# An order model that waits for the eighth-preceding transfer, and keeps a lock for each of two engines (linear attention and MLP, one core)

## Chip, cores and metric

The kernel runs on one core of one Trainium2 chip. The metric is the device time of one execution in microseconds (us). Before the change the median of three runs was 403.05 us (402.95 to 403.12).

The engines are named as in the profile: PE is TensorE (PEld its weight loads), DVE is VectorE, ACT is ScalarE, POOL is GpSimd, SP is SyncE, which here issues nearly all transfers (DMA).

## What is computed

A block whose output is the input plus two branches of its normalised form: linear attention with 32 heads of 16, and an MLP with squared ReLU. The sequence is 2048 long, the width 512, the MLP's width 1376; all is f32.

```python
def _A_ref(x, wqkv, wo):                    # q, k, v: (heads, S, 16)
    ...
    phi = lambda t: jnp.where(t > 0, t + 1, jnp.exp(t)) + 1e-6
    pq, pk = phi(q), phi(k)
    kv = jnp.einsum("bhsd,bhse->bhde", pk, v)
    z = jnp.einsum("bhsd->bhd", pk)
    num = jnp.einsum("bhqd,bhde->bhqe", pq, kv)
    den = jnp.einsum("bhqd,bhd->bhq", pq, z)[..., None] + 1e-6
    ...
def _B_ref(x, w1, b1, w2, b2):
    h = jnp.einsum("bsd,df->bsf", x, w1) + b1
    ...
    h = r * r                                # r = max(h, 0)
    out = jnp.einsum("bsf,fd->bsd", h, w2) + b2
...
x = A_x
xn = _layernorm(x, axis=-1)
return x + _A_ref(xn, A_wqkv, A_wo) + _B_ref(xn, B_w1, B_b1, B_w2, B_b2)
```

## The kernel before

**Work.** Tokens go in 16 tiles of 128, four to a block of 512. Each f32 product is made of a high and a low part of either operand and three matmuls, high by high, low by high and high by low; names that end in h and l are such parts (xs0h, xs1l, wkh, wkl). Most of the MLP is multiplied in a form with seven products in place of eight, for which sums and differences of weights are made on chip, written to DRAM (wd1, wd2, wdz) and read back (ops). In the first 105 us the 16 token tiles pass one after the other: statistics (st, mv, y) and normalisation (xp) on DVE, a turn of the tile, the key projection into PSUM (ps), phi of it (k, then pk, whose high half is made on ACT and whose low half on DVE), and the product of pk with the tokens, split into halves as well (tok, ACT and POOL), summed in acc. A number behind the name is that of the tile: k9 belongs to tile 9.

The first eight tiles are turned by TensorE and stored for later use (xTd, from t). The others take another way: DVE writes the normalised tiles of four (xp8, xp12), SP sends them through 16 small transfers to xg (xg8, xg12: each line of the order is 32 partitions by 512 numbers), and DVE turns each with a STREAM_TRANSPOSE into xT, whose halves are xs0h/xs0l or xs1h/xs1l. wv is the value weight, a megabyte, loaded through SP too.

**Order.** Nothing is issued when the program text runs. Each call on an engine is caught by a `Recorder` and kept by `Program.add` as a task with an estimated duration. `Program.order` (line 183) then searches for an order: `play` (line 269) runs a list scheduler over a model of the engines, in which each engine takes the ready task with the earliest due date; `press` (line 254) moves due dates ahead for tasks before which TensorE stood idle in the model; 500 such rounds run from each of the seven seeds in `STARTS`, and then the due dates of stretches of the results are crossed. `emit` (line 340) issues the tasks of the best order; so one line, 343, stands for all instructions in the profile. TensorE's own order is that of the text and is not searched; the first tasks of all engines (`fixed`) are as written, too.

Two things in the model matter here. `t.lock` marks sums (tensor_tensor and scalar_tensor_tensor on DVE without a PSUM operand, tensor_tensor on POOL): one number, `locked`, lets none of them start before the end of the last one, on whichever engine. And a transfer (`t.size` above 0) takes its place behind the previous ones in one stream, `dma`, and its readers wait for its landing, `t.lag` later. How many transfers are under way is not limited in the model. In the program as built each SP or ACT transfer signals one of eight semaphores, in turn, and waits for the one before it on the same semaphore.

Of the kernel before, what the change touches and what calls it, by code (L numbers as in the profile page):

```python
# [79 lines left out]
class Program:  # L80
# [96 lines left out]

    ENGINES = ("tensor", "vector", "scalar", "gpsimd", "sync")
    DEEP, FAR = 4.0, 15.0
    STARTS = (0, 1, 3, 5, 6, 7, 8)  # L180
    ROUNDS = 500

    def order(self):
# [36 lines left out]
        plain, best, found = [t.due for t in ts], None, []  # L220
        for start in self.STARTS:
            chance, back = random.Random(start), (8, 16, 4)[start % 3]
# [46 lines left out]
    def play(self):  # L269
        ts, engines, inf = self.tasks, self.ENGINES, float("inf")  # L270
        free = dict.fromkeys(engines, 0.0)
        later = {e: [] for e in engines}
        now = {e: ([], []) for e in engines}
        lane, at, before = self.lanes, dict.fromkeys(engines, 0), dict.fromkeys(engines)
        when = dict.fromkeys(engines, inf)
        locked, dma, last = 0.0, 0.0, 0.0
        push, pop = heapq.heappush, heapq.heappop

        def look(e):
            row = lane[e]  # L280
            if at[e] < len(row):
                t = row[at[e]]
                when[e] = inf if t.left else max(free[e], t.ready)
            elif now[e][0] or now[e][1]:
                when[e] = free[e]
            else:
                when[e] = max(free[e], later[e][0][0]) if later[e] else inf

        for t in ts:
            t.left, t.ready, t.cause = len(t.preds), 0.0, None  # L290
            if not t.left and not t.placed:
                push(later[t.engine], (0.0, t.index, t))
        for e in engines:
            look(e)
        done = 0
        while done < len(ts):
            e = min(engines, key=when.get)
            begin = when[e]
            if at[e] < len(lane[e]):
                t = lane[e][at[e]]  # L300
                at[e] += 1
            else:
                wait, (easy, hard) = later[e], now[e]
                while wait and wait[0][0] <= begin + 0.1:
                    t = pop(wait)[2]
                    push(hard if t.lock else easy, (t.due, t.index, t))
                if hard and (not easy or hard[0] < easy[0] and locked <= begin + 0.1):
                    t = pop(hard)[2]
                else:
                    t = pop(easy)[2]  # L310
                    if t.size and dma > begin + self.DEEP and t.due > begin + self.FAR:
                        push(wait, (dma - self.DEEP / 2, t.index, t))
                        look(e)
                        continue
            done += 1
            t.start, t.behind = max(begin, t.ready), before[e]
            before[e] = t
            if t.lock:
                t.start = max(t.start, locked)
                locked = t.start + t.dur  # L320
            end = t.start + t.dur
            free[e] = end - t.skip
            last = max(last, end)
            if t.size:
                dma = end = max(dma, end) + t.size / 300e3
            for s, lag in t.follow:
                ready = end + lag
                if ready >= s.ready:
                    s.ready, s.cause = ready, t
                s.left -= 1  # L330
                if not s.left:
                    o = s.engine
                    if not s.placed:
                        push(later[o], (s.ready, s.index, s))
                    if o != e:
                        look(o)
            look(e)
        return last
# [1384 lines left out]
```

## Time and profile before

| | before |
|---|---|
| median of three runs | 403.05 us |
| the profiled execution | 403.15 us |
| its span, first to last instruction | 401.3 us |
| granted TensorE clock, mean | 1.000 |
| PE busy | 393.5 us, 1769 matmuls, 98% |
| DVE busy | 351.0 us, 565 instructions, 87% |
| ACT busy | 271.7 us, 475 instructions, 68% |
| POOL busy | 59.1 us, 73 instructions, 15% |

A row of the timeline is read so: start and duration in us, engine, line, operation, output and inputs by the program's names (tile numbers left out), their shape and how many instructions the row stands for; in brackets how long the engine stood idle before it and what ended the wait. SPq is SP's queue while it issues a transfer. A row of the chain of waits is start, duration and what the time was spent on. The span leaves out 1.85 us of the profiled execution.

### The profile page before, as it was taken

What the parts mean: (1) busy time and instruction counts of PE and PEld (TensorE: products, weight loads), DVE (VectorE), ACT (ScalarE), POOL (GpSimd) and SP (SyncE); (2) the same over time, 40 slices, a digit from 0 to 9 for tenths busy, and PEclk for the clock granted to TensorE, in tenths of its full rate; (3) what the DMA queues carried; (4) which work ended last, traced back from release to release, by engine and by line L of the source; (5) the groups of instructions that cost most, each with busy time, mean ns of one, the idle gap of its engine ahead of it and who ended that gap; (6) DMA issues with size and microseconds to landing.
All of it is one profiled execution on the core that took longest, in us unless ns stands there. A gap on an engine that the chain in (4) does not pass through costs nothing.

```text
span 401.3 us, 5606 instructions
## 1 busy us (share of the span) xinstructions
PE 393.5 (98%) x1769; PEld 325.4 (81%) x1769; DVE 351.0 (87%) x565; ACT 271.7 (68%) x475; POOL 59.1 (15%) x73
## 2 busy tenths in 40 slices
PE   7999999999999999999999999999999999999994
PEld 6778887888888888888888888888888888888883
DVE  6899979899898999999889989988999989676884
ACT  5776776666769989999747552277958677455440
POOL 2232324540213424300000000030000000000000
PEclk9999999999999999999999999999999999999999
DMA  7872654876499898589446799989998599989434
GB/s 229 297 221 61 166 155 186 281 275 244 148 314 296 324 340 310 235 292 313 179 140 193 246 259 224 363 240 295 265 239 272 186 227 296 236 266 275 158 65 93
DMA packets 80177, 94.36 MB, mean 235 GB/s; under 512 B 39410, under 2 KB 50674, under 8 KB 79892
## 3 DMA queue, kind: packets, MB, share of 16 engines
q1 hardware_dynamic: 78964, 93.49, 76.0%
q10 hardware_dynamic: 1088, 0.26, 0.4%
q0 software_dynamic: 96, 0.26, 0.3%
q8 instruction: 14, 0.23, 0.2%
q14 instruction: 15, 0.12, 0.1%
HBM read 57.55 MB, written 34.34 MB: 229 GB/s over the span
## 4 chain that ended last, share of the span: by engine, by line
PE 86%; DVE 6%; DMA 3%; SPq 1%; issue 1%; ACT 1%; DVEq 0%; ACTq 0%
PE ps L343 50%; PE acc L343 36%; DMA wv<-in_A_wqkv_dram 2%; SPq L343 1%; DVE xp L343 1%; DVE st L343 1%; DVE y L343 1%; DMA x<-in_A_x_dram 1%; DVE xs0l L343 1%; DMA xg<-xp 0%; DVE pk L343 0%; DVE k L343 0%; DVE res L343 0%; DVE o L343 0%; DVE ops L343 0%
## 5 line engine op out<-in xcount | busy, mean ns | idle before, releaser
L343 PE MATMUL ps<-s,ops 128*128 128x512 f32 x429 | 101.0, 389 | 0.0
L343 PEld LDWEIGHTS ps<-s,ops 128*128 128x128 f32 x429 | 80.5, 188 | 16.7
L343 PE MATMUL acc<-s,ops 128*128 128x512 f32 (+1 forms) x222 | 51.0, 381 | 0.0
L343 ACT ACTIVATE s<-rr 128x512 fp32r<-128x512 f32 x56 | 34.9, 630 | 22.9 <-DVE s L343 10.9
L343 DVE TENSOR_TENSOR s<-rr,s 128x512 fp32r<-128x512 f32 x56 | 39.0, 706 | 10.5 <-ACT s L343 9.6
L343 PE MATMUL acc<-pk,tok 128*128 128x512 f32 x192 | 47.2, 394 | 0.2 <-ACT pk L343 0.2
L343 PEld LDWEIGHTS acc<-s,ops 128*128 128x128 f32 x222 | 40.5, 188 | 8.2 <-ACT s L343 0.3
L343 PEld LDWEIGHTS acc<-pk,tok 128*128 128x128 f32 x192 | 35.4, 188 | 8.5 <-POOL tok L343 0.6
L343 PE MATMUL acc<-T,ops 128*128 128x512 f32 x168 | 41.2, 389 | 0.0
L343 PE MATMUL ps<-T,ops 128*128 128x512 f32 x168 | 40.9, 390 | 0.0
L343 PEld LDWEIGHTS acc<-T,ops 128*128 128x128 f32 x168 | 31.5, 188 | 6.6
L343 PEld LDWEIGHTS ps<-T,ops 128*128 128x128 f32 x168 | 31.5, 188 | 6.5
L343 POOL TENSOR_TENSOR tok<-xp,tok 128x512 fp32r<-128x512 f32 x16 | 22.4, 1398 | 28.2 <-ACT tok L343 20.5
L343 PE MATMUL ps<-xs0h,ops 128*128 128x512 f32 x72 | 23.6, 389 | 0.0
L343 POOL TENSOR_TENSOR ops<-s,ops 128x512 fp32r<-128x512 f32 x12 | 16.7, 1395 | 36.6 <-ACT ops L343 36.2
L343 ACT ACTIVATE rr<-acc 128x512 f32<-128x512 f32 x23 | 13.5, 591 | 10.8 <-PE acc L343 10.8
L343 DVE STREAM_TRANSPOSE d<-d 128x1024 f32<-128x1024 f32 x16 | 19.8, 1236 | 0.2
L343 POOL DMA_DIRECT2D out_dram<-res x2 | 1.5, 729 | 122.5 <-DVE res L343 120.0
L343 PE MATMUL acc<-xs0h,ops 128*128 128x512 f32 x56 | 18.4, 389 | 0.0
L343 POOL TENSOR_TENSOR made<-t,made 128x512 fp32r<-128x512 f32 x2 | 3.1, 1559 | 98.5 <-issue 97.4
L343 ACT ACTIVATE rr<-rr,odds 128x512 f32<-128x512 f32 x15 | 10.8, 722 | 9.6 <-DVE rr L343 9.6
L343 DVE TENSOR_TENSOR rr<-acc,rr 128x512 f32<-128x512 f32 x21 | 14.3, 687 | 2.7 <-PE acc L343 1.3
(181 smaller groups left out, 811.7 us busy)
## 6 DMA issues: line engine op xcount, KB each, us to landing
ops<-wd SPq DMA_DIRECT2D x77, 256.0 KB, 4.6
wd<-ops SPq DMA_DIRECT2D x35, 512.0 KB, 3.7
ops<-wd SPq DMA_DIRECT2D x23, 512.0 KB, 5.9
wd<-ops SPq DMA_DIRECT2D x25, 256.0 KB, 4.0
res<-in_A_x_dram SPq DMA_DIRECT2D x32, 128.0 KB, 6.1
out_dram<-res SPq DMA_DIRECT2D x26, 128.0 KB, 3.5
ops<-wdz SPq DMA_DIRECT2D x6, 512.0 KB, 6.1
x<-in_A_x_dram SPq DMA_DIRECT2D x5, 512.0 KB, 6.2
```

The costliest lines, as they stand in the source:

```text
L343: getattr(getattr(self.nc, t.engine), t.name)(*map(real, t.args), **{k: real(a) for k, a in t.kw.items()})
```

## The change

The starts of the search go from seven seeds to one, another. The model's lock becomes one for each of the two engines, and a sum waits for the lock of the other engine alone, so that DVE's sums no longer wait in the model for each other. A transfer of SP or ACT does not start in the model before the eighth-preceding one has landed. The tasks, their number, their dependences and the order of TensorE are as before.

```diff
-    STARTS = (0, 1, 3, 5, 6, 7, 8)
+    STARTS = (2,)
...
-        locked, dma, last = 0.0, 0.0, 0.0
+        locked, dma, last = {"vector": 0.0, "gpsimd": 0.0}, 0.0, 0.0
+        other = {"vector": "gpsimd", "gpsimd": "vector"}
+        landed = [0.0] * 8
...
-                if hard and (not easy or hard[0] < easy[0] and locked <= begin + 0.1):
+                if hard and (not easy or hard[0] < easy[0] and locked[other[e]] <= begin + 0.1):
...
             if t.lock:
-                t.start = max(t.start, locked)
-                locked = t.start + t.dur
+                t.start = max(t.start, locked[other[e]])
+                locked[e] = t.start + t.dur
+            if t.size and e != "gpsimd":
+                t.start = max(t.start, landed[-8])
             end = t.start + t.dur
...
             if t.size:
                 dma = end = max(dma, end) + t.size / 300e3
+                if e != "gpsimd":
+                    landed.append(end + t.lag)
```

The diff tells nothing of the order that comes out. It differs on DVE, ACT, POOL and SP from about 24 us on, save the last dozen instructions of each. Three places follow; a number at a name's end counts tiles of the pool, and differs between the two programs without meaning.

DVE, around the keys of tile 9 (k9, pk9), beside the turning of tiles 12 and 13 (xT3 from xg12). Before:

```order
L343 STREAM_TRANSPOSE xT3_757<-xg12_624 128x4x4x32
L343 TENSOR_TENSOR ops_753<-t1_0_718,ops_753 128x2x256
L343 TENSOR_TENSOR xs1l_174<-xT2_636,xs1h_165 128x4x128
L343 TENSOR_TENSOR xs0l_404<-xT3_757,xs0h_393 128x4x128
L343 SCALAR_TENSOR_TENSOR k9_769<-ps3_70,k9_769 128x512
L343 STREAM_TRANSPOSE xT3_757<-xg12_624 128x4x4x32
L343 TENSOR_TENSOR t2_0_810<-raw_2_2_314 128x256
L343 SCALAR_TENSOR_TENSOR pk9_804<-k9_769,pk9_804 128x512
```

The same place now:

```order
L349 STREAM_TRANSPOSE xT3_760<-xg12_631 128x4x4x32
L349 TENSOR_TENSOR ops_427<-raw_2_1_306,ops_427 128x256
L349 TENSOR_TENSOR xs1l_174<-xT2_652,xs1h_165 128x4x128
L349 SCALAR_TENSOR_TENSOR k9_771<-ps3_70,k9_771 128x512
L349 TENSOR_TENSOR xs0l_402<-xT3_760,xs0h_392 128x4x128
L349 STREAM_TRANSPOSE xT3_760<-xg12_631 128x4x4x32
L349 SCALAR_TENSOR_TENSOR pk9_793<-k9_771,pk9_793 128x512
```

k9 moved ahead of the xs0l sum, and the sum behind the first transpose is another, of half the size. On ACT, pk9's high half now follows k9 at once; before, tok11 stood between them. On DVE near 24 us (not shown) one of two BN_AGGR that stood ahead of xp4's normalisation moved behind it, beside the other.

SP, from the stores of the turned tiles 4 to 7 (xTd1) to the first stores of made weights (wd2_1). Before:

```order
L343 DMA xTd1_78<-t4_400 512x1x128
L343 DMA xg8_474<-xp8_429 32x512 x16
L343 DMA xTd1_78<-t5_472 512x1x128
L343 DMA wv_604<-in_A_wqkv_dram 128x4x512
L343 DMA xg12_624<-xp12_575 32x512 x4
L343 DMA xTd1_78<-t6_549 512x1x128
L343 DMA xg12_624<-xp12_575 32x512 x12
L343 DMA xTd1_78<-t7_628 512x1x128
L343 DMA wd2_1_87<-ops_421 128x512 x2
```

Now:

```order
L349 DMA xTd1_78<-t4_399 512x1x128
L349 DMA xTd1_78<-t5_472 512x1x128
L349 DMA xg8_503<-xp8_430 32x512 x16
L349 DMA xTd1_78<-t6_544 512x1x128
L349 DMA xg12_631<-xp12_564 32x512 x16
L349 DMA xTd1_78<-t7_621 512x1x128
L349 DMA wd2_1_87<-ops_419 128x512 x2
L349 DMA wv_746<-in_A_wqkv_dram 128x4x512
```

wv moved from between xg8 and xg12 behind both, and the store of t5 ahead of xg8. On DVE the first xp8 normalisations, which xg8 reads, stand later: a statistics instruction (BN_STATS) for tile 7 and one for tile 12, xs0l and k4 are now ahead of the second of them.

ACT, in the MLP, around the relu and square of one tile (c21, then s0_2_1, its high half). Before:

```order
L343 ACTIVATE h0_1498<-h0_1498 128x512
L343 ACTIVATE ops_1554<-raw_1_4_1253 128x256
L343 ACTIVATE c21_2_1566<-ps0_67,odds_105 128x512
L343 ACTIVATE c21_2_1566<-c21_2_1566 128x512
L343 ACTIVATE rf2_1434<-ps1_68 128x512
L343 ACTIVATE s0_2_1_1581<-c21_2_1566 128x512
```

Now:

```order
L349 ACTIVATE h0_1498<-h0_1498 128x512
L349 ACTIVATE d1_1555<-rr0_1_1294,odds_105 128x512
L349 ACTIVATE c21_2_1562<-ps0_67,odds_105 128x512
L349 ACTIVATE ops_1566<-raw_1_4_1258 128x256
L349 ACTIVATE c21_2_1562<-c21_2_1562 128x512
L349 ACTIVATE rf2_1438<-ps1_68 128x512
L349 ACTIVATE s0_2_1_1581<-c21_2_1562 128x512
```

The 128x256 copy (ops from raw) moved from ahead of the relu to behind it, and d1, which came later, stands ahead of it.

## The prediction

> **What bounds the kernel now.** I read the page's busy times first, where TensorE is busy for 98% of the span, then busy time by stretch of the span.
>
> ```profile
> PE 393.5 (98%) x1769; PEld 325.4 (81%) x1769; DVE 351.0 (87%) x565; ACT 271.7 (68%) x475; POOL 59.1 (15%) x73
> ```
>
> ```profile
> 7.70:66.00 58.30, 58.13 (x266) 46.97 (x265) 52.71 (x113) 41.51 (x87) 19.77 (x30) 1.00 0.62 189
> 66.00:70.00 4.00, 3.78 (x17) 2.80 (x17) 3.90 (x9) 3.62 (x7) 0.36 (x1) 1.00 0.20 81
> 70.00:150.00 80.00, 80.00 (x370) 66.65 (x369) 72.72 (x109) 62.69 (x109) 24.07 (x20) 1.00 0.80 277
> ...
> 395.90:401.30 5.40, 0.02 (x1) 0.00 (x0) 0.95 (x3) 0.20 (x1) 0.00 (x0) 0.98 0.49 97
> ```
>
> The columns are the stretch, its length, then busy time and count for PE, weight loads, DVE, ACT and POOL, the granted clock, the DMA share and GB/s. From 7.70 to 395.90 TensorE has work without a visible hole but for 0.17 us before 66 and 0.22 us behind it; the stretches left out read like that of 70 to 150, full. The clock is 1.00 in all of them, so it leaves nothing to win. VectorE is 87% busy and never the bound in a whole stretch. TensorE's order is fixed, so the body can give back only the moments at which an operand came late. A shared row of matmuls hides small ones, because each matmul is drawn longer than its place in the pipeline. The chain of waits gives the step: a row of twelve in 2.72 us is 0.227 each. With it the PE timeline can be checked for lateness:
>
> ```profile
> 69.67 2.72 PE ps L343 x12
> ```
>
> ```profile
> 24.98 1.07 PE L343 MATMUL ps<-wkh,xs1l 128*128 128x512 f32 x4
> 26.22 0.66 PE L343 MATMUL ps<-ident,xp 128*128 128x128 f32 x4 [0.17 <-DVE xp L343]
> ...
> 65.38 1.07 PE L343 MATMUL ps<-wkh,xs1l 128*128 128x512 f32 x4
> 66.67 3.00 PE L343 MATMUL acc<-pk,tok 128*128 128x512 f32 x12 [0.22 <-ACT pk L343]
> 69.51 0.39 PE L343 MATMUL ps<-wkh,xs1h 128*128 128x512 f32 x1
> ...
> 149.07 0.39 PE L343 MATMUL ps<-xs1h,ops 128*128 128x512 f32 x1
> 149.30 3.01 PE L343 MATMUL acc<-s,ops 128*128 128x512 f32 x12
> 152.15 1.07 PE L343 MATMUL ps<-T,ops 128*128 128x512 f32 x4
> ```
>
> The four matmuls from 65.38 are over at 65.38 + 4 × 0.227 = 66.29; the next block starts at 66.67, **0.38 late**, and takes 69.51 − 66.67 = 2.84 instead of 2.72, another 0.12: **0.50 us** together, the largest stall of the body. At 26.22 it is 26.22 − 25.89 = 0.33. The block at 149.30 takes 2.85, 0.13 too long. What else I find by this step are four single delays of about 0.1 before 22 us, where the orders of both programs agree. All in all, 0.50 + 0.39 (26.22 and its short block) + 0.13 + 0.4, they come to some 1.4 us: the most that a new order can win in the body. It can lose without such a bound.
>
> **The change part by part.** No instruction is added or removed, and the order of the matmuls is the same; the eight semaphores on which transfers really wait are in both programs, so the eighth-preceding wait is new in the model alone and has no cost on the chip. [...] What changes are rows on DVE, ACT, POOL and SP. The first rows (to about 24 us) and the last dozen of every engine are word for word alike, so the 7.7 us at the start and the 5.4 us at the end stay.
>
> *The stall at 66.67.* What came late there:
>
> ```profile
> 45.60 7.48 DMA wv<-in_A_wqkv_dram
> ...
> 58.73 1.97 DMA xg<-xp
> ```
>
> ```profile
> 60.82 0.71 DVE L343 STREAM_TRANSPOSE xT<-xg 128x512 f32<-128x512 f32 x1 [1.78 <-DMA xg<-xp]
> ...
> 61.00 1.29 POOL L343 TENSOR_TENSOR tok<-xp,tok 128x512 fp32r<-128x512 f32 x1
> 61.46 1.39 DVE L343 TENSOR_TENSOR ops<-t,ops 128x512 fp32r<-128x512 f32 x1
> ...
> 62.58 0.67 ACT L343 ACTIVATE ops<-t 128x512 fp32r<-128x512 f32 x1
> 62.77 0.68 DVE L343 TENSOR_TENSOR xs1l<-xT,xs1h 128x512 fp32r<-128x512 f32 x1
> 63.15 0.62 ACT L343 ACTIVATE k<-k 128x512 f32<-128x512 f32 x1
> 63.33 1.32 POOL L343 TENSOR_TENSOR ops<-t,ops 128x512 fp32r<-128x512 f32 x1 [1.00 <-ACT ops L343]
> ...
> 63.37 1.83 DVE L343 TENSOR_TENSOR xs0l<-xT,xs0h 128x512 fp32r<-128x512 f32 x1
> ...
> 64.60 1.76 POOL L343 TENSOR_TENSOR tok<-xp,tok 128x512 fp32r<-128x512 f32 x1
> ...
> 65.12 0.68 DVE L343 SCALAR_TENSOR_TENSOR k<-ps,k 128x512 f32<-128x512 f32 x1
> ...
> 65.89 0.63 ACT L343 ACTIVATE pk<-k 128x512 fp32r<-128x512 f32 x1 [1.43 <-DVE k L343]
> ```
>
> The wv load held the transfer queue for 7.48 us, the last xg12 piece landed at 60.70, and from there DVE had five operations before k, two of them long: a sum of two SBUF tiles takes 0.68 alone, and 1.39 or 1.83 when it meets a POOL sum; it ends about 0.56 after POOL's (62.85 after 62.29, 65.20 after 64.65). The k operation, which reads PSUM, ran its 0.68 inside POOL's 64.60 to 66.36. In the new order k9 stands ahead of the xs0l sum, the sum ahead of it is half as wide, and on ACT pk9 stands ahead of tok11. Worked forward, from a transpose that starts at 60.82 as now: the 128x256 sum waits for POOL till 62.29 and ends at 62.6; xs1l starts at 62.5. **Lower end:** it runs 0.68; k9 then waits for its exponential, which stands one 0.5 us step earlier on ACT (63.77 before, 63.25 now), runs to 63.95, and pk9 ends at 64.7. **Upper end:** POOL's ops sum, whose ACT input also comes earlier, starts at 62.4 ahead of xs1l and ends at 63.7; xs1l ends at 64.26, k9 at 64.9, pk9 at 65.6. TensorE took its block 0.15 after pk ended (66.52 to 66.67) and lost 0.12 more in it, so pk9 is in time if it ends by 66.29 − 0.15 − 0.12 = 66.02. Both ends are, by 1.3 and by 0.4 us. I take the stall as gone: **−0.50**. The bounds are −0.50 and, if the landing is late, what the slower case below costs.
>
> That landing has its own change. wv moves behind all 32 xg pieces, so its 7.48 us hold nothing there, but xp8 is normalised later: two statistics, xs0l and k4 now stand ahead.
>
> ```profile
> 34.72 10.11 SPq L343 DMA_DIRECT2D xg<-xp  x16
> ```
>
> ```profile
> 29.68 1.48 DVE L343 TENSOR_SCALAR xp<-x,mv,y 128x512 f32<-128x512 f32 x1
> ...
> 35.80 1.28 DVE L343 BATCH_NORM_STATS2 st<-x 128x6 f32<-128x512 f32 x2
> ...
> 39.65 0.55 DVE L343 TENSOR_SCALAR xp<-x,mv,y 128x512 f32<-128x512 f32 x1
> ```
>
> ```profile
> 36.52 1.29 POOL L343 TENSOR_TENSOR tok<-xp,tok 128x512 fp32r<-128x512 f32 x1 [3.57 <-DVE st L343]
> ```
>
> The first xg8 piece left at 34.72. With 1.28 for the statistics and 0.6 each for xs0l and k4 it leaves at 37.2; if POOL's tok sum (36.52 to 37.81) holds a normalisation, at 38.1. I take the later. Sixteen pieces took 10.11, 0.632 each, so 32 of them with one xTd store (0.57) end at 38.1 + 20.2 + 0.6 = 58.9; the last leaves at 58.3 and lands, with 1.97, near **60.3 to 60.5**, against 60.70. What was won by moving wv is nearly spent by the late start; I count nothing for the 0.2 to 0.4 that are left.
>
> *26.22.* The xp normalisation that ended it waited behind this row:
>
> ```profile
> 24.25 0.16 DVE L343 BATCH_NORM_AGGREGATE mv<-st 128x2 f32<-128x6 f32 x1
> 24.33 0.66 DVE L343 BATCH_NORM_STATS2 st<-x 128x6 f32<-128x512 f32 x1
> ```
>
> Now the aggregate stands behind xp4. Its step is 24.33 − 24.25: **−0.08**. Bounds 0 and −0.16, its full length.
>
> *149.30.* On ACT a 128x256 copy moves behind the relu c21, and d1, a wide activation, in front of it.
>
> ```profile
> 145.41 0.42 ACT L343 ACTIVATE ops<-raw 128x256 fp32r<-128x256 f32 x1 [0.33 <-PE acc L343]
> 146.77 0.69 ACT L343 ACTIVATE c<-ps,odds 128x512 f32<-128x512 f32 x1 [0.94 <-PE ps L343]
> 147.50 0.63 ACT L343 ACTIVATE c<-c 128x512 f32<-128x512 f32 x1
> ```
>
> The copy ran in idle time (0.94 before the relu). Now relu ends at 147.46, the copy's step of about 0.3 follows, and the square starts near 147.7 instead of 147.50. The operation behind the square began only at its end, 148.13, so about 0.1 is swallowed there, and s is 0.1 later: **+0.10**; bounds 0 and the whole 0.42. d1 fits in the idle time. If that cover were gone it would cost its 0.7.
>
> *318.* One ACT copy of acc passes the s1_4_1 activation:
>
> ```profile
> 316.99 0.63 ACT L343 ACTIVATE s<-rr 128x512 fp32r<-128x512 f32 x1
> 317.53 0.58 ACT L343 ACTIVATE rr<-acc 128x512 f32<-128x512 f32 x1
> ```
>
> ```profile
> 318.13 1.52 PE L343 MATMUL ps<-s,ops 128*128 128x512 f32 x6
> ```
>
> s ended at 317.62, 0.51 before its matmul; with the copy (about 0.5 from start to start) ahead of it, just in time. I take **+0.05**, between 0 and, if 0.2 of that room is needed to load the weights, 0.2.
>
> *Elsewhere.* Of the moved loads at 231 to 257, two ops loads go ahead of res loads, which feeds TensorE earlier; no load was waited for there before, so the value is 0, and res is needed only for output rows.
>
> **Sum:** −0.50 − 0.08 + 0.10 + 0.05 = −0.43. The profiled execution took 403.15, of which the span is 401.3 and 1.85 lies around it; so 402.72, span near 400.9. The median of 403.05 is 0.10 below the profiled execution: **402.6**.
>
> **The rivals.** *Slower: the late start of xg8 grows.* Place: the three xp8 normalisations on DVE and behind them the SP queue. In the rows above one takes 0.55 alone and 1.48 against a POOL sum, 0.93 more. I have put one such hold in (38.1). Each further one makes the last landing, and with it pk9, 0.93 later, against a margin of 0.4 in the worse case. It decides from an xg8 start of 38.5 on: one more hold gives a stall of 0.53, as large as the one removed, and 403.1; two more give 1.46 and **404.1**. For it: DVE is nearly always busy there (52.71 of 58.30). Against: POOL has one tok sum in that time, 36.52 to 37.81, and its next comes behind an ACT copy.
>
> *No change.* The stall at 66.67 is shortened only, because something that I left in place ends last: POOL's tok or DVE's low half of pk, which also feed that block. Then 0.2 to 0.5 comes back: 402.8 to 403.3, middle **403.05**. For it: DVE's own pk came at 66.65 plus 0.68, with room of some tenths only. The case that the change does nothing on the chip, since the wait was there anyway, gives the same number; the moved rows speak against it.
>
> [...]
>
> *Faster than forecast.* All lateness goes: 1.4 − 0.5 more, at most **401.7**. It would need the first 22 us to change, whose rows are alike.
>
> **How the numbers follow.** The forecast has 0.50 and a range of its own of 402.3 to 402.85; no change 0.22; slower 0.17; faster than forecast 0.11. A measurement of this kernel tells a difference from about 0.2%, 0.8 us: below 402.24 or above 403.86. Below it lie the last case and 0.03 of the forecast's: 0.14. Above it, 0.12 of the slower case. The rest is 0.74. The range of 402.0 to 403.9 leaves out half of the last case and 0.11 of the slower one, some 0.17.
>
> **What would show it.** In the changed profile: the PE block acc<-pk,tok near 66.3 without idle time before it and 2.72 long; k ahead of xs0l on DVE, pk ending before 66.0; the first xg8 issue near 38 and the last xg12 landing near 60.4; wv behind them; the relu's block near 148.8 still some 0.2 late. PE busy from 7.7 to about 395.4. It would be wrong if xg lands after 61, if PE shows a new releaser above 0.2 us, or if DMA appears among what PE waits for.

## The result, and the profile after

| | before | with the change |
|---|---|---|
| median | 403.07 us (10 runs, 402.75 to 403.19) | **404.94 us** (10 runs, 403.28 to 406.57) |
| the profiled execution | 403.15 us | 405.0 us |
| its span | 401.3 us | 403.3 us |
| the body: TensorE from its first key projection to the end of its last matmul | 388.19 us | 390.13 us |

The ratio is 1.0043, with an interval of 1.0028 to 1.0058: slower by 0.4%, where 402.6 us was forecast. The span grew by 2.0 us, of which 1.94 lie in the body; head and tail are as they were. The runs spread more as well, by 3.3 us against 0.4 for the ten of the kernel before. That is weak evidence by itself: beside the experiments below, on three other occasions, the kernel before spread by 1.0, 2.9 and 1.3 us.

Busy time in one stretch of the span, before and then with the change (stretch, length, then PE, weight loads, DVE, ACT, POOL, the clock, the DMA share, GB/s):

```profile
250.00:350.00 100.00, 100.00 (x443) 82.74 (x442) 90.14 (x127) 68.08 (x112) 3.12 (x2) 1.00 0.94 262
```

```profile
250.00:350.00 100.00, 99.14 (x436) 81.09 (x435) 85.51 (x121) 67.38 (x110) 3.33 (x2) 1.00 0.92 251
```

The clock is 1.00, so nothing was lost there. The stretch held 443 matmuls and now holds 436. Seven matmuls at 0.227 are 1.59 us. What PE waited for, profile of the changed kernel (us in total, times, longest):

```profile
PE acc L349 <- ACT rr L349: 0.9, 2, 0.6
PE acc L349 <- ACT pk L349: 0.2, 1, 0.2
```

The second line is the stall at 66, which was to go. The first is new. PE's timeline there:

```profile
268.00 3.00 PE L349 MATMUL acc<-T,ops 128*128 128x512 f32 x12
271.21 1.66 PE L349 MATMUL acc<-T,ops 128*128 128x512 f32 x6 [0.21 <-ACT rr L349]
272.71 0.39 PE L349 MATMUL acc<-xs1h,ops 128*128 128x512 f32 x1
...
273.84 0.39 PE L349 MATMUL acc<-xs1h,ops 128*128 128x512 f32 x1
274.88 1.66 PE L349 MATMUL acc<-T,ops 128*128 128x512 f32 x6 [0.65 <-ACT rr L349]
276.38 0.39 PE L349 MATMUL acc<-xs0h,ops 128*128 128x512 f32 x1
```

By the step of 0.227 the twelve from 268.00 are over at 270.72, so the block at 271.21 is 0.49 late; 273.84 + 0.227 = 274.07, so the one at 274.88 is 0.81 late; and each of the two takes 1.50 instead of 1.36. Together 0.49 + 0.81 + 0.28 = **1.58 us**, most of the loss. (The brackets show less, 0.21 and 0.65, since a row of matmuls is drawn past its end: the twelve are drawn 3.00 long, and step in 2.72.) Both blocks waited for an ACT copy, rr<-acc, which empties the bank of acc that they write to: the two waits of 0.9 in all above (rr are tiles of sums taken out of acc, d and e are made from them on ACT). Back along that wait, timelines of ACT, DVE and POOL of the changed kernel:

```profile
268.73 0.81 ACT L349 ACTIVATE d<-rr,odds 128x512 f32<-128x512 f32 x1 [0.91 <-DVE rr L349]
269.45 0.71 ACT L349 ACTIVATE e<-rr,odds 128x512 f32<-128x512 f32 x1
270.07 0.61 ACT L349 ACTIVATE hz<-hz 128x512 f32<-128x512 f32 x1
270.59 1.06 ACT L349 ACTIVATE rr<-acc 128x512 f32<-128x512 f32 x2
...
274.25 0.58 ACT L349 ACTIVATE rr<-acc 128x512 f32<-128x512 f32 x1
```

```profile
253.62 1.22 DVE L349 TENSOR_TENSOR xT<-xT,xT 128x1024 f32<-128x1024 f32 x1
256.97 0.69 DVE L349 TENSOR_TENSOR res<-o,res 128x512 f32<-128x512 f32 x1 [2.12 <-DMA ops<-wd]
...
266.28 2.41 DVE L349 SCALAR_TENSOR_TENSOR rr<-rr,e 128x512 f32<-128x512 f32 x2
```

```profile
266.54 3.33 POOL L349 TENSOR_TENSOR made<-t,made 128x512 fp32r<-128x512 f32 x2 [98.35 <-issue]
```

The copies at 270.59, for the first block, stand behind d, e and hz on ACT; the copy at 274.25, for the second, hangs on them in turn, through a DVE sum at 271.19 and the e that follows it. The d at 268.73 waited 0.91 for DVE's pair of rr sums, which took 2.41 while POOL's two sums ran (in e_no_wait below, nearly clear of them, such a pair took 1.28). And DVE itself had stood still for **2.12 us at 256.97**, at the third sum into res. res is the residual input, loaded in the layout of the output by eight small transfers; four DVE sums add a transposed result to it, and nothing but the output reads it.

The bracket names an ops transfer, which the sum does not read. In the trace the sum waits for four of the eight semaphores that the transfers share, those of the last four loads of res (103, 104, 105 and 109), and the ops transfer signals one of these four later. So the name settles nothing; the time at which the loads of res landed does. The last load of the changed kernel, then the last two of the kernel before (duration of the issue, when issued; time to landing):

```profile
L349 SPq DMA_DIRECT2D res<-in_A_x_dram x1: 1899/1899/1899, 246.0 to 246.0; - x1
...
DMA to landing us min/median/max: 10.8/10.8/10.8
```

```profile
L343 SPq DMA_DIRECT2D res<-in_A_x_dram x2: 312/1052/1793, 242.5 to 243.4; - x2
...
DMA to landing us min/median/max: 10.6/10.6/10.6
```

With the change the last load landed at 246.0 + 10.8 = 256.8, just ahead of the sum; before, at 243.4 + 10.6 = 254.0, and the sums that need it began here, without a wait:

```profile
256.13 1.25 DVE L343 TENSOR_TENSOR res<-o,res 128x512 f32<-128x512 f32 x2
```

The margin was 2.1 us. The new order issues the last load 2.6 us later, as two ops loads go ahead of it, and has DVE ready for the sum at 254.85, 1.3 earlier: together 3.9.

### The profile page after: what moved, and what is told of

Read it like the earlier page. It is cut to its first block, busy times and chain, and to the rows that moved or that the text cites. A ratio compares the mean times of both kernels' runs of the same rounds, so it can differ in the third digit from the quotient of the medians.

```text
span 403.3 us, 5611 instructions
## 1 busy us (share of the span) xinstructions
PE 395.4 (98%) x1769; PEld 325.8 (81%) x1769; DVE 352.4 (87%) x565; ACT 270.9 (67%) x475; POOL 58.2 (14%) x73
## 4 chain that ended last, share of the span: by engine, by line
PE 70%; DMA 6%; DVE 4%; ACT 2%; issue 0%; SPq 0%; ACTq 0%
PE ps L349 41%; PE acc L349 29%; DMA res<-in_A_x_dram 4%; DMA ops<-wd 2%; DVE rr L349 1%; DVE res L349 1%; DVE o L349 1%; ACT rr L349 0%; DVE t L349 0%; ACT d L349 0%; SPq L349 0%; DVE s L349 0%; DVE xs1l L349 0%; DVE T L349 0%; ACT e L349 0%
## 5 line engine op out<-in xcount | busy, mean ns | idle before, releaser
L349 PE MATMUL ps<-s,ops 128*128 128x512 f32 x429 | 101.1, 390 | 0.0
L349 PEld LDWEIGHTS ps<-s,ops 128*128 128x128 f32 x429 | 80.5, 188 | 16.9 <-ACT s L349 0.3
L349 PE MATMUL acc<-s,ops 128*128 128x512 f32 (+1 forms) x222 | 51.0, 381 | 0.0
L349 DVE TENSOR_TENSOR s<-rr,s 128x512 fp32r<-128x512 f32 x56 | 38.4, 692 | 13.8 <-ACT s L349 13.5
L349 ACT ACTIVATE s<-rr 128x512 fp32r<-128x512 f32 x56 | 34.9, 629 | 21.3 <-DVE s L349 10.2
L349 PE MATMUL acc<-pk,tok 128*128 128x512 f32 x192 | 47.2, 395 | 0.2 <-ACT pk L349 0.2
L349 PEld LDWEIGHTS acc<-s,ops 128*128 128x128 f32 x222 | 40.5, 188 | 8.3 <-ACT s L349 0.3
L349 PE MATMUL acc<-T,ops 128*128 128x512 f32 x168 | 41.7, 392 | 0.9 <-ACT rr L349 0.9
L349 PEld LDWEIGHTS acc<-pk,tok 128*128 128x128 f32 x192 | 35.4, 188 | 8.4 <-issue 0.6
L349 PE MATMUL ps<-T,ops 128*128 128x512 f32 x168 | 41.0, 390 | 0.0
L349 PEld LDWEIGHTS acc<-T,ops 128*128 128x128 f32 x168 | 31.3, 188 | 8.3 <-ACT rr L349 1.7
L349 PEld LDWEIGHTS ps<-T,ops 128*128 128x128 f32 x168 | 31.5, 188 | 6.5
L349 POOL TENSOR_TENSOR tok<-xp,tok 128x512 fp32r<-128x512 f32 x16 | 22.7, 1421 | 31.5 <-ACT tok L349 22.9
L349 PE MATMUL ps<-xs0h,ops 128*128 128x512 f32 x72 | 23.7, 390 | 0.0
L349 ACT ACTIVATE rr<-acc 128x512 f32<-128x512 f32 x23 | 13.4, 587 | 12.7 <-PE acc L349 12.5
L349 DVE STREAM_TRANSPOSE d<-d 128x1024 f32<-128x1024 f32 x16 | 19.7, 1237 | 1.5 <-ACT d L349 1.4
L349 POOL TENSOR_TENSOR ops<-s,ops 128x512 fp32r<-128x512 f32 x12 | 16.7, 1393 | 30.0 <-ACT ops L349 28.1
L349 POOL DMA_DIRECT2D out_dram<-res x2 | 1.5, 729 | 124.7 <-DVE res L349 122.1
L349 DVE TENSOR_TENSOR ops<-raw,ops 128x512 fp32r<-128x512 f32 (+1 forms) x22 | 18.1, 828 | 0.5 <-ACT ops L349 0.5
L349 PE MATMUL acc<-xs0h,ops 128*128 128x512 f32 x56 | 18.4, 389 | 0.0
L349 ACT ACTIVATE rr<-rr,odds 128x512 f32<-128x512 f32 x15 | 10.8, 721 | 11.1 <-DVE rr L349 11.1
L349 POOL TENSOR_TENSOR made<-t,made 128x512 fp32r<-128x512 f32 x2 | 3.3, 1690 | 98.3 <-issue 98.3
```

What stands on the lines that cost most here:

```text
L349: getattr(getattr(self.nc, t.engine), t.name)(*map(real, t.args), **{k: real(a) for k, a in t.kw.items()})
```

## The experiments

In all kernels but the four that begin with a_, the order is one of the two programs', edited by hand as shown (+ and - against the kernel named); those four take what the search gives. All compute the full result. Where a ratio stands, it is to the kernel before, run beside it. L398 is the line that issues everything in these kernels, as L343 and L349 are in the two programs.

**Taking the loads ahead** (e_res_early; the changed order, SP).

```diff
 DMA res<-in_A_x_dram 32x16x64
+DMA res<-in_A_x_dram 32x16x64 x3
 DMA ops<-wdz 128x1024
 DMA ops<-wd1_0 128x1024
-DMA res<-in_A_x_dram 32x16x64 x3
 DMA ops<-wd1_1 128x1024 x2
```

> The changed order with one edit on SP: the last three res3 loads go ahead of two ops loads (wdz, wd1_0) that stand before them. Theory A (VectorE's wait of 2.12 us at 257 for the last res3 load is what makes TensorE late at 271 and 275): the loads land near 253.5 instead of 256.8, the wait at 257 is gone, no wait of PE on ACT rr is left, and the time is 403.1 +- 0.3 instead of 404.9, with runs within 0.5 us of each other. Theory B (ACT's order and POOL's hold make the stall whatever the loads do): the wait at 257 is gone too, but PE still waits for ACT rr at 271 to 275 by over 1 us, and the time stays above 404.3.

Measured: 403.6 us (402.93 to 404.16), 1.0013 with an interval of 1.0004 to 1.0021, clear of that of the change; body 389.26 in the slowest of the eleven runs, which is the profiled one. The wait at 257 and both stalls behind it are gone, though the two ops loads went later: so the loads of res were what held DVE, and the stalls hung on that. The time is 0.2 above the range expected, and the runs lie 1.2 apart, not 0.5. A smaller wait came 8 us earlier, at the first of the four sums, in the timeline of DVE:

```profile
248.94 0.69 DVE L398 TENSOR_TENSOR res<-o,res 128x512 f32<-128x512 f32 x1 [1.96 <-DMA res<-in_A_x_dram]
```

It cost PE 1.0 us of idle time at 257.65, again through an ACT copy rr<-acc.

**Changing ACT's order instead** (e_copy_first; the changed order, ACT).

```diff
 ACTIVATE d<-rr0,odds 128x512
+ACTIVATE rr1<-acc 128x512 x2
 ACTIVATE d<-rr0,odds 128x512
 ACTIVATE e<-rr0,odds 128x512
 ACTIVATE hz<-hz 128x512
-ACTIVATE rr1<-acc 128x512 x2
```

> The changed order with one edit on ACT: the two copies of acc into rr1_1, for which TensorE waits at 271, go ahead of d, e and hz, three operations that need VectorE's late results. Theory A in its narrow form (the late VectorE reaches TensorE only through these three operations on ACT): the wait of 2.1 us at 257 stays, but the stall at 271 (0.6 us) is gone and that at 275 becomes under 0.5; time 403.3 to 404.0. If VectorE's lateness reaches TensorE by itself as well (its own reads of acc): stalls of 1 us or more remain, 404.2 or more.

Measured: 406.85 us (405.81 to 409.45), 1.0108 (1.0084 to 1.0132). The narrow form of the theory missed, and its other case came: with the copies first the stall moved and grew. What PE waited for:

```profile
PE acc L398 <- ACT rr L398: 1.4, 1, 1.4
...
PE acc L398 <- DVE rr L398: 0.5, 1, 0.5
```

DVE stood for 2.76 at the same res sum, and its rr results came late for PE directly. So another place for the copies does not help while the wait stands. More than that the run does not show, since the edit also put e later, for which a DVE sum then waited 1.57 instead of 0.90.

**Both halves of DVE's wait** (e_no_wait; e_res_early, and on DVE the sums T3 and xT1, which need no transfer, ahead of the four res sums).

```diff
 TENSOR_TENSOR T<-xT,T 128x1024
+TENSOR_TENSOR T3<-xT,T3 128x1024
+TENSOR_TENSOR xT1<-xT1,xT 128x1024
 STREAM_TRANSPOSE o<-m 128x512
 TENSOR_TENSOR res<-o,res 128x512
...
-TENSOR_TENSOR T3<-xT,T3 128x1024
-TENSOR_TENSOR xT1<-xT1,xT 128x1024
 TENSOR_TENSOR res<-o,res 128x512
```

> The changed order with two edits: on SP the last three res3 loads ahead of the two ops loads, as in e_res_early, and on VectorE T3 and xT1 (2.3 us of work) ahead of the four res3 sums, which so start later. e_res_early only moved the wait: the first res sum waited 1.96 us at 249 for the fourth load. Theory A (VectorE, in order, stands at a res sum for a load that has not landed, and what is queued behind it feeds TensorE): VectorE then waits for no res load by over 0.3 us, PE waits for no ACT rr between 250 and 280, and the time is 403.0 to 403.4, runs within 0.7 us. Theory B (the changed order has too little room at 257 to 275 by itself): VectorE waits for no load and PE still waits for ACT rr by 0.5 us or more; 403.7 or more.

Measured: 403.6 us (403.19 to 403.98), 1.0006 (0.9994 to 1.0018); body 388.87, that is 1.26 less than with the change. The time is 0.2 above the range expected, and the ratio flatters it: the kernel before, with a median of 403.17, had runs up to 405.49 beside it. No res sum waits, and PE has no wait for a copy. DVE, ACT and PE where the changed kernel stalled:

```profile
264.84 1.28 DVE L398 SCALAR_TENSOR_TENSOR rr<-rr,e 128x512 f32<-128x512 f32 x2
```

```profile
268.81 0.58 ACT L398 ACTIVATE rr<-acc 128x512 f32<-128x512 f32 x1
270.00 0.60 ACT L398 ACTIVATE rr<-acc 128x512 f32<-128x512 f32 x1 [0.60 <-PE acc L398]
```

```profile
268.44 4.24 PE L398 MATMUL acc<-T,ops 128*128 128x512 f32 x18
```

These rows of DVE and ACT stand in the same order in both kernels. The rr pair starts 1.44 earlier than with the change (264.84 against 266.28) and POOL's sums do not hold it (1.28 against 2.41): 2.57 us in all, nearly half of it a collision into which the wait had pushed it. The copy ends ahead of PE's need, and the 18 matmuls run through. Of the 0.68 by which the body is still longer than before, 0.30 stand near 52.8; the rest are single tenths.

**The two halves of the order** (e_first_half: the changed order up to about 210 us, behind it that of the kernel before).

> The changed order up to about 210 us, then the order of before. If all of the loss lies in the second half, as the trace says (PE waits at 271 and 275): 403.0 to 403.4, with the stall at 67 of about 0.45 still there and one of 0.16 at 52.7. If the loss were of the whole program (a search from one start, transfers in other places), over 404.

Measured: 403.38 us (403.06 to 405.19), 1.0012 (1.0003 to 1.0021); body 387.91. The loss of 1.9 sits behind 210 us; ahead of it are some tenths at most. The stall at 66 is under 0.2 in this profile, where about 0.45 was expected.

**The early part** (e_fixed: e_no_wait, and the xp8 normalisations and the first xg8 transfer as early as in the kernel before).

```diff
 (DVE)
+TENSOR_SCALAR xp8<-x,mv,y 128x4x128
 BN_STATS st<-x 128x6
 ...
+TENSOR_SCALAR xp8<-x,mv,y 128x4x128 x2
 BN_STATS st<-x 128x6
 TENSOR_TENSOR xs0l<-ps,xs0h 128x4x128
 SCALAR_TENSOR_TENSOR k4<-ps,k4 128x512
-TENSOR_SCALAR xp8<-x,mv,y 128x4x128
 BN_AGGR mv<-st 128x2 x2
-TENSOR_SCALAR xp8<-x,mv,y 128x4x128 x2
 (SP)
+DMA xg8<-xp8 32x512 x16
 DMA xTd1<-t5 512x1x128
-DMA xg8<-xp8 32x512 x16
```

> e_no_wait with the early part mended too: on VectorE the three later xp8 normalisations stand as early as in before (ahead of xs0l and k4), on SP the store of t5 goes behind the 16 xg8 pieces. If the stalls left in e_no_wait at 52.6 (0.30) and 66.5 (0.45) come from the late start of xg8 (38.3): xg8 starts near 35, xg12 lands before 59, both stalls are gone, PE's body from its first projection to its end is near 388.0 and the time is 402.6 to 403.0. If they come from something else (the load of instructions at 47, POOL's hold on xs1l): the stall at 66.5 stays within 0.2 of 0.45, 403.2 to 403.6.

Measured: 403.16 us (402.9 to 403.5), 1.0000 (0.9991 to 1.0009); body 387.92. The time is 0.2 above the range expected; the body and the stalls are as foreseen. PE has no stall at 52.6, and its block at 66 came on time:

```profile
65.39 1.07 PE L398 MATMUL ps<-wkh,xs1l 128*128 128x512 f32 x4
66.30 2.88 PE L398 MATMUL acc<-pk,tok 128*128 128x512 f32 x12
```

With the late res loads, the res sums and the late start of xg8 undone, the time is that of the kernel before.

**k9 alone** (e_k9: the kernel before, with two of the change's moves).

```diff
 (DVE)
+SCALAR_TENSOR_TENSOR k9<-ps,k9 128x512
 TENSOR_TENSOR xs0l<-xT,xs0h 128x4x128
-SCALAR_TENSOR_TENSOR k9<-ps,k9 128x512
 (ACT)
+ACTIVATE pk9<-k9 128x512
 ACTIVATE tok11<-xp 128x4x4x32
-ACTIVATE pk9<-k9 128x512
```

> The order of before with the first term of the prediction alone: k9 ahead of the xs0l sum on VectorE and pk9 ahead of tok11 on ACT. If the prediction's working of that place was right and only the landing of xg12 was wrong: the PE block at 66.67 starts at 66.3, the stall of 0.50 is gone, and the time is 402.5 +- 0.2 (-0.5). If the working was wrong itself (POOL's hold, or pk's low half): 402.8 to 403.2 and the stall is there.

Measured: 403.15 us (402.86 to 404.1), 1.0006 (0.9997 to 1.0014), no gain. The profiled execution, the fastest of the eleven, has no stall at 66 and a body of 387.69, 0.50 less than before. Why the median is no lower, the **control** suggests, the kernel before itself once more:

> The kernel before once more, its order given as a list, no edit: a second profile of it. If the stall at 66.67 belongs to every execution: PE's body is 388.1 to 388.3 as in the first profile and a stall of 0.4 to 0.5 stands near 66. If it depends on when the transfers land in that execution (then removing it can gain no 0.5 in the median): a body of 387.6 to 388.0 and a smaller stall.

403.2 us. PE's timeline of that execution, at 66 and at 254:

```profile
65.42 1.07 PE L398 MATMUL ps<-wkh,xs1l 128*128 128x512 f32 x4
66.33 2.90 PE L398 MATMUL acc<-pk,tok 128*128 128x512 f32 x12
...
254.63 1.98 PE L398 MATMUL acc<-T,ops 128*128 128x512 f32 x8
256.85 0.47 PE L398 MATMUL acc<-xs1h,ops 128*128 128x512 f32 x1 [0.25 <-DMA ops<-wd]
```

The block at 66.33 came 65.42 + 0.91 = 66.33, on time. The stall of 0.50 on which the forecast rests is not in every execution of the kernel before; this one lost about as much at 257 (254.63 + 8 × 0.227 = 256.45, so 0.40), to an ops load. So the missing stall of e_k9 proves nothing by itself. What the two moves do shows in the high half of pk9 on ACT, in e_k9 and then in the control:

```profile
64.12 0.63 ACT L398 ACTIVATE pk<-k 128x512 fp32r<-128x512 f32 x1 [0.82 <-DVE k L398]
```

```profile
65.44 0.63 ACT L398 ACTIVATE pk<-k 128x512 fp32r<-128x512 f32 x1 [0.94 <-DVE k L398]
```

They bring its end from 66.07 to 64.75, 1.3 us. The control was in time without them, as its last xg piece landed at 60.26 (60.23 in e_k9); in the first profile of before it landed at 60.70, and pk9 ended at 66.52.

**The parts of the change.** The search was run with one lock for each engine alone (a_lock), with the wait for the eighth-preceding transfer alone (a_land), with both and the seven old seeds (a_both), and with the one new seed alone in the old model (a_start). Each gives an order of its own.

> The search of before with the separate locks alone (old seeds, no eighth-preceding wait). In its order the res3 loads stay as early as before (last one issued near 241), but the third res sum stands 5 us earlier than before. Theory A: a wait of 1 to 2 us on a res load near 252 and a time of 403.4 to 404.6. If the locks are harmless: 402.6 to 403.2.

402.67 us (402.45 to 403.55), 0.9988 (0.9978 to 0.9998): no slower than before, in the range for harmless locks. One of its res sums waits as well, in DVE's timeline, but no wait of PE follows:

```profile
251.97 0.69 DVE L398 TENSOR_TENSOR res<-o,res 128x512 f32<-128x512 f32 x1 [1.36 <-DMA res<-in_A_x_dram]
```

The wait was foreseen; the loss expected from it did not come. It is shorter (1.36) and 5 us earlier than with the change, and DVE, which reached its rr sums at 258.12, was in time for PE.

> The search of before with the eighth-preceding wait alone. Its res3 loads go late (behind two more ops loads, as in the changed order), but VectorE's res sums stand where they did before. Theory A: the last loads land near 256.5 and the sum that needs them is due near 256.4, so a wait of 0 to 0.7 us and 402.9 to 403.5. If late loads alone make the loss: over 404.

405.71 us (405.2 to 406.86), 1.0064 (1.0049 to 1.008); a miss. A res sum did wait, for 0.97 at 260, but PE lost hardly more than 0.1 behind it. The loss has another place, at 150: a sum on DVE took 1.75 while a POOL sum ran, where one of the same size took 0.67 two rows later (152.73), and PE waited 1.76 for it (see the last section).

> Both edits of the model with the seven seeds of before. Its order has the late loads and the early sums together, like the changed one. Theory A: a wait of about 2 us on a res load at 255 to 257 and 404 to 405.5. If the one seed is what costs: 402.6 to 403.3.

403.15 us, but from 402.46 to 407.67 in 12 runs, 1.0021 (0.9992 to 1.0049). Seven runs end by 403.21 and five lie at 404.43 or above, so the median lies in the range expected if the one seed is what costs, and only two runs in that of 404 to 405.5. The profiled one took 404.61, with a body of 389.85. What DVE and PE waited for in it:

```profile
DVE res L398 <- DMA res<-in_A_x_dram: 2.7, 2, 2.1
```

```profile
PE acc L398 <- ACT rr L398: 1.6, 2, 1.0
```

The same chain as with the change, in an order from other seeds: followed back, PE's second wait, at 274.53, begins at a load of res that landed at 256.05. None of the seven was profiled.

> The search of before with the one seed alone (2 in place of seven), old lock, no eighth-preceding wait. The search's own end is 1.3 us later than with seven seeds. If the model's end carries over to the chip: 403.8 to 404.8. If what the chip does is decided by transfers that the model times by itself: anywhere from 402.6 to 406, and a stall of TensorE at a place where the model has none.

405.16 us (404.98 to 405.6), 1.0048 (1.0036 to 1.0061), 0.4 above the first range expected and inside the second, which leaves out little. One seed gives a worse order by itself, and there is no wait at res in it. Its body is 389.71. About 0.7 is lost at 149, and as much at 271, where the changed kernel stalled too and PE waits 0.5 for ACT's rr. DVE and POOL ahead of that:

```profile
266.86 4.13 DVE L398 SCALAR_TENSOR_TENSOR rr<-rr,e 128x512 f32<-128x512 f32 x3
```

```profile
266.60 3.24 POOL L398 TENSOR_TENSOR made<-t,made 128x512 fp32r<-128x512 f32 x2 [98.04 <-issue]
```

Here the three rr sums met POOL's and took 4.13, where two took 1.28 in e_no_wait, with no wait for a transfer ahead of them, and ACT's d then waited 0.91 for DVE. So the change's loss has no single line of the diff behind it, and a wait at res is neither needed for a loss nor enough for one: a_lock has one and loses nothing, a_start loses without. At 271, as far as these runs go, it depends on when DVE gets to its rr sums in the order that comes out, against PE's need and POOL's sums; with the change the wait at res made it late.

**A better order** (e_lock_late; the order of a_lock, with the sums T3 and xT1 on DVE ahead of the res sum that waited there).

> a_lock, the fastest so far, with T3 and xT1 ahead of the third res sum on VectorE, so that its wait of 1.36 us for a res load at 252 is filled with work. No stall of PE hung on that wait in the profile, so the median should stay at 402.5 to 402.8; if the slower executions of a_lock (up to 403.55) come from that wait growing, they become fewer and the highest is under 403.2. If T3 and xT1 were needed later than what they now push back: 403 or more.

**402.65 us** (402.53 to 402.71 in 11 runs), 0.9985 (0.9977 to 0.9994): faster than both kernels, by 0.15% than the one before. The gain is that of a_lock (402.67); what is new is that no res sum waits and that the runs lie within 0.18 us, where those of a_lock lay 1.1 apart. That the edit did this is not shown, since the two were run on different chips, on which the kernel before spread by 2.9 and 1.3. The same sum in its timeline of DVE:

```profile
252.93 0.68 DVE L398 TENSOR_TENSOR res<-o,res 128x512 f32<-128x512 f32 x1
```

## Why the prediction was wrong

*Elsewhere: the step that failed.* The prediction gave the loads moved at 231 to 257 the value 0, because no load was waited for there before and "res is needed only for output rows". The first half holds for TensorE, whose operands did come in time. The second looked at who needs the result, and not at the engine that makes it: in the profiles of both programs all 565 rows of DVE stand in the order of the program, so a sum whose product nobody is waiting for still holds back the rr sums behind it, ACT's d behind those, the copies behind d, and PE behind the copies. Four links later an output-only load was worth 1.58 us. Both sides of that sum had moved, the loads 2.6 us later and DVE 1.3 earlier, against a margin of 2.1, which stood in the profile of before; that both would move, and which way, stood in the two orders. e_res_early shows that the wait is the head of the chain, and e_no_wait that PE's stalls go with it.

*The stall at 66.67: −0.50 forecast, 0 found.* The moves do what was forecast: in e_k9, which has them alone, pk9 ends 1.3 us earlier than in the control. (Between the landing and k, DVE had four operations in the profile of before, not five.) The stall was there with the change because the landing was later than forecast. SP, POOL, DVE, ACT and PE of the changed kernel:

```profile
38.29 11.30 SPq L349 DMA_DIRECT2D xg<-xp  x16
...
50.37 10.07 SPq L349 DMA_DIRECT2D xg<-xp  x16
```

```profile
63.45 1.44 POOL L349 TENSOR_TENSOR ops<-t,ops 128x512 fp32r<-128x512 f32 x1
```

```profile
62.10 0.71 DVE L349 STREAM_TRANSPOSE xT<-xg 128x512 f32<-128x512 f32 x1 [1.19 <-DMA xg<-xp]
...
63.63 1.80 DVE L349 TENSOR_TENSOR xs1l<-xT,xs1h 128x512 fp32r<-128x512 f32 x1
65.36 0.68 DVE L349 SCALAR_TENSOR_TENSOR k<-ps,k 128x512 f32<-128x512 f32 x1
```

```profile
66.07 0.63 ACT L349 ACTIVATE pk<-k 128x512 fp32r<-128x512 f32 x1 [1.45 <-DVE k L349]
```

```profile
65.57 1.07 PE L349 MATMUL ps<-wkh,xs1l 128*128 128x512 f32 x4
66.85 3.01 PE L349 MATMUL acc<-pk,tok 128*128 128x512 f32 x12 [0.21 <-ACT pk L349]
69.70 0.39 PE L349 MATMUL ps<-wkh,xs1h 128*128 128x512 f32 x1
```

The first xg8 piece left at 38.29, as forecast (38.1). But the first sixteen took 11.30 instead of 10.11, and the last piece landed at 61.88 instead of 60.3 to 60.5. From there the upper end held: xs1l met POOL's sum and took 1.80 (0.68 in the profile of before, between two of POOL's), pk ended at 66.70, PE started 0.15 behind it. 66.85 − 66.48 = 0.37 late, and 2.85 − 2.72 = 0.13 in the block: 0.50 again. The price is the slower rival's 0.53; its cause, a second hold of a normalisation, is not what happened. And as a term of the median it was mis-sized: the control did not pay it, and with the moves alone the median did not fall.

*The small terms.* At 149 the block of twelve is 0.05 later than the row ahead of it allows, forecast +0.10; at 318, 0.13 in the block, forecast +0.05; at 26, a few hundredths won, forecast 0.08. New is 0.16 at 52.6, where the later xg8 kept DVE's transposes 1.57 waiting. Together with the 1.58 this makes 1.9 of the body's 1.94.

*The range.* The slower rival was given its place at xg8, with the right sort of cause, a transfer that comes late for DVE; its bound of 404.1 knew one such transfer only, though the prediction says itself that a new order can lose without a bound. Two of its three signs of being wrong came: xg landed after 61, and PE has a new releaser, ACT's rr, with 0.9 us. The third, a DMA among what PE waits for, did not come and was no test: the wait was at DVE.

## What to carry to other kernels

Where an order changes, list for each engine whose rows stand in the order of the program, as all of DVE, ACT, POOL and SP do in the profiles of both programs here, every instruction that waits for a transfer, also those whose result nobody hurries for, with its margin in us (landing against the time at which the engine is ready), before and after. Here a margin of 2.1 us was lost to moves of 2.6 and 1.3, and in the two profiled executions of the kernel before one and the same transfer landed up to 1.9 us apart. What depends on it is all that stands behind it on that engine, so put work that needs no transfer ahead of such an instruction: with T3 and xT1 there and the loads as early as in e_res_early, e_no_wait had no wait at a res sum, and none of PE for a copy. And a stall seen in one profile is a gain only if the next profile of the same kernel has it as well.

## What was not expected of the hardware

*The clock after a stall.* In a_land, PE stood 1.76 us before the second row below, and the granted clock fell to 0.56 over the next 3.4 us. PE's timeline and the stretches:

```profile
149.30 1.20 PE L398 MATMUL acc<-s,ops 128*128 128x512 f32 x4
152.26 3.52 PE L398 MATMUL acc<-s,ops 128*128 128x512 f32 x8 [1.76 <-DVE s L398]
155.57 1.75 PE L398 MATMUL ps<-T,ops 128*128 128x512 f32 x6
```

```profile
152.20:155.60 3.40, 3.34 (x9) 2.62 (x10) 3.03 (x6) 0.93 (x2) 0.00 (x0) 0.56 0.92 325
```

The block began 152.26 − 150.21 = 2.05 late, and its eight matmuls took 3.31 us in place of 1.82, another 1.49: 3.5 of the 3.73 that the body lost. A stall that begins a block 1.55 late by the same reckoning, in e_copy_first, left the clock at 1.00. The other five runs of a_land were shorter, at a mean clock of 0.997 to 1.000 against 0.992, so the drop probably belongs to this execution; they were not profiled. The longest runs of e_copy_first (407.77 and 409.45 us) and of a_both (407.16 and 407.67) list 0.992 or 0.993 as well, so they may hold such a drop too. What sets it off is not shown. DMA moved nothing in the gap of a_land either (0 GB/s from 150.0 to 152.2, and 324 from 273.0 to 275.5 around the stall of e_copy_first); whether that has to do with it was not tried.

*Landings.* A load of res took 10.6 to 11.5 us from its issue to its landing around 245, in the profiles of before and after, where an xg piece took 2.0 around 60; and the fourth load of res landed at 248.73 in e_res_early and at 245.13 in e_no_wait, where SP's whole order is the same and only DVE's differs. In the two executions of the kernel before that were profiled, the loads of res landed 1.0 us apart at most. Whether such differences make the spread of 3.3 us is not shown: of the orders in which no res sum waits, e_lock_late spread by 0.18, e_fixed by 0.6 and e_no_wait by 0.8.

*A transfer of instructions.* Why the first sixteen xg pieces took 1.2 longer is not settled. One issue among them, near 47.2, took 1.78 instead of 0.59, and a piece landed 3.3 us after its issue instead of 2.0, while 16 KB of instructions were loaded on another queue. The same load stands near 47 in the profiles of e_no_wait and e_first_half, and there, too, one issue took 1.93 and 1.34 and the first sixteen 11.44 and 10.86. In the kernel before it falls into the 7.48 us of wv. The two fell together; nothing more is shown.
